# An S4 convolution and SwiGLU kernel: its order from the first feed-forward product on laid out by a planner in the source, and block products summed by accumulating transfers

## The chip, the core and the metric

The kernel runs on one core of a Trainium2 chip. A core has a matrix engine (TensorE, in the profile PE, its weight loads PEld), three engines for elementwise work (VectorE, in the profile DVE; ScalarE, ACT; GpSimd, POOL) and a queue engine that issues transfers (SyncE, SP). Sixteen DMA engines move data between the device memory and the on-chip memory, and within the latter. Each engine works through its own instructions in order and waits on semaphores for the others. The metric is the device time of one execution in microseconds.

## The reference

The input of 2048 rows by 512 features goes through two layers. Each adds a long convolution of the normalized rows, and then a gated feed-forward of the normalized result. Weights are the same in both layers.

```python
def _A_ref(u, A_re, A_im, B_re, B_im, C_re, C_im, log_dt, Dskip):
    dt = jnp.exp(log_dt)[:, None]
    logdA, dB = dt * (A_re + 1j * A_im), dt * (B_re + 1j * B_im)
    P = jnp.exp(logdA[:, :, None] * l[None, None, :])
    K = jnp.einsum("dn,dnl,dn->dl", Cc, P, dB).real
    ...
    Yf = Uf * Kf[None, :, :, :]
    y = irfft(Yf)[:L]
    return y + u * Dskip

def _B_ref(x, w_gate, w_up, w_down):
    return (silu(x @ w_gate) * (x @ w_up)) @ w_down

x = x + _A_ref(_layernorm(x), ...)
x = x + _B_ref(_layernorm(x), ...)
x = x + _A_ref(_layernorm(x), ...)
x = x + _B_ref(_layernorm(x), ...)
```

## The kernel before

The 2048 rows are four blocks of 512. With two layers there are eight block steps, in the order `SEQ`: (0,0), (0,1), (0,2), (1,0), (0,3), (1,1), (1,2), (1,3), as (layer, block). The text calls them step 0 to step 7. A step needs the spectra of the earlier blocks of its own layer, and for layer 1 the output of layer 0 for its block.

The first part, some 329 us, makes the convolution's kernel from its parameters, its spectra (`wdr` in device memory for the earlier blocks, `w0r` on chip for a block with itself), the spectra of blocks 0 and 1 of layer 0, and the convolution of step 0. DVE, ACT and PE stand there in the order of the source (`manual_schedule`). The change leaves this part as it is, up to the splitting of the feed-forward weights.

From the first feed-forward product on, each step has two halves of work.

The convolution (`ssm`, `forward`). A block is normalized, folded into lanes, and turned into spectra by products with a constant matrix (`pf`, line 276), which ACT copies to `u` (line 278); POOL stores them to `udr` (line 706) for later blocks. There are eight units per step: two halves of the features by four residues q. A unit multiplies its own spectrum by `w0r`, and that of each earlier block, loaded as `uu`, by a loaded `w`: one DVE product per block (line 755), each of 128 x 1024 numbers, and one DVE addition for each earlier block (line 758). Then come the joining of real and imaginary parts (lines 759 and 760), the split into a high and a low half-precision part (ACT line 763, DVE line 232), the products back (`pi`, line 774), and the combination of four units into the rows (`t1`, `t2`, `xt`, lines 791 to 807).

The feed-forward (`ffn`, `ffn_norm`, `remainder`). 256 rows at a time: a half block. The rows are normalized (ACT lines 223 to 226, a power on POOL line 227, DVE line 228), split into high and low parts and transposed by SP's transfers (line 840). Five groups of 48 products of 256 columns (`pgu`, lines 885 to 887) and one smaller group for the remaining 96 columns (lines 852 to 854) make gate and up. Each group is evicted by four instructions, in turns on ACT and DVE (lines 890 to 893). Then the second product `py` follows, two rows of 128 with 33 products each (lines 899 to 901); each row is added to `xt` by DVE (line 904) and stored by SP (line 906). `pgu` and `py` share two buffers of tag `big`.

Every product is made of three half-precision ones (high by high, high by low, low by high). So the weights are split too: ACT writes the high part (lines 641 and 667), DVE the low part (lines 646 and 670). These splits run on into the first feed-forward.

In this part the source gives only a program order. The framework's scheduler, with a timeline of its own, orders the instructions of every engine; evictions and the convolution's products have a raised priority (`BOOST`).

Of the kernel before, what the change touches and what calls it, by code (L numbers as in the profile page):

```python
# [11 lines left out]
F32 = mybir.dt.float32  # L12
# [29 lines left out]
HALF = 2  # L42
INV = 1
# [38 lines left out]
def kernel(ctx, tc, x, a_re, a_im, b_re, b_im, c_re, c_im, log_dt, d_skip,  # L82
# [10 lines left out]
                xf=1, nn=1, hh=1, hl=1, sg=2, hf=1, stats=2, stats2=2, ef=1)  # L93
# [38 lines left out]
    w0r = sb.tile([P, 2, 4, 2, HD], F32, name="w0r")  # L132
# [106 lines left out]

    def norm_x(n):  # L240
        rs, nb = row_stats(n, 4, 1.0, "stats", lambda r: tl([P, D], "junk", "t1", BF16))
        for c in range(4):
            A.activation(n[:, c], n[:, c], AF.Identity, scale=rs[:, c:c + 1], bias=nb[:, c:c + 1])

    def forward(n, h, eh):


        hs = slice(h * HD, (h + 1) * HD)
        x0, x1, x2, x3 = (n[:, c, hs] for c in range(4))
        bt = tl([P, 7, HD], "bt", "bt")  # L250
        a_, b_, p_, q_, r_, s_, hx = (bt[:, i] for i in range(7))
        stt(a_, x2, HH, x0, OP.add)
        stt(b_, x2, -HH, x0, OP.add)
        A.activation(hx, x2, AF.Copy, scale=HH)
        stt(p_, x3, TT, x1, OP.add)
        stt(r_, x3, -TT, x1, OP.add)
        stt(q_, x1, TT, x3, OP.subtract)
        stt(s_, x1, TT, x3, OP.add)
        for i, q in enumerate(QORD):
            z = z2[:, 0 if eh else i % 2]  # L260
            u_, v_ = ((p_, a_) if q in (0, 3) else (q_, b_))
            stt(z[:, 0], u_, CC if q < 2 else -CC, v_, OP.add)
            stt(z[:, 1], s_ if q in (0, 3) else r_, CC, hx, OP.add if q < 2 else OP.subtract)
            if eh:
                hl = z2[:, 1].bitcast(F16).rearrange("p i (l d) -> p l i d", l=2)
                A.activation(hl[:, 0], z, AF.Copy, scale=256.0)
                stt(hl[:, 1], z, 256.0, hl[:, 0], OP.subtract)
            pf = psml([P, 2, HD], "pf")
            with tc.high_priority(offset=BOOST):
                for o in range(2):  # L270
                    if eh:
                        terms = [(eh[:, q, o + i, le], hl[:, lz, i]) for i in range(2) for le, lz in ((0, 0), (0, 1), (1, 0))]
                    else:
                        terms = [(ef[:, q, o + i], z[:, i]) for i in range(2)]
                    for k, (e, m) in enumerate(terms):
                        PE.matmul(pf[:, o], lhsT=e, rhs=m, start=k == 0, stop=k == len(terms) - 1)  # L276
                u = tl([P, 2, HD], "u", "u")
                A.activation(u, pf, AF.Copy, scale=2.0 ** -16 if eh else 1.0)  # L278
            yield q, u
# [400 lines left out]
    def inputs():  # L680

        for layer, b in SEQ:
# [160 lines left out]
    def remainder(pgu, nh, nlo, hh, hl):  # L843

        rows = TB // P
        fs = slice(F - FR, F)
        pr = pgu.rearrange("p a b t -> p (a b t)")[:, :rows * 2 * FR].rearrange("p (r w f) -> p r w f", r=rows, w=2)
        for r in range(rows):
            rc = slice(r * P, (r + 1) * P)
            for wi in range(2):  # L850
                for k in range(4):
                    PE.matmul(pr[:, r, wi], lhsT=nh[:, k, rc], rhs=wgu(wi, k, 0)[:, fs], start=k == 0, stop=False)
                    PE.matmul(pr[:, r, wi], lhsT=nh[:, k, rc], rhs=wgu(wi, k, 1)[:, fs], start=False, stop=False)
                    PE.matmul(pr[:, r, wi], lhsT=nlo[:, k, rc], rhs=wgu(wi, k, 0)[:, fs], start=False, stop=k == 3)
        with tc.high_priority(offset=BOOST):
            both = tl([P, 2, TB], "sgr", "sg")
            sg = both[:, 0, :rows * FR].rearrange("p (r f) -> p r f", r=rows)
            hs = both[:, 1].bitcast(F16).rearrange("p (l r f) -> p l r f", l=2, r=rows)
            G.memset(hs[:, :, :, FR:], 0.0)
            A.activation(sg, pr[:, :, 0], AF.Silu, scale=sc6[:, 3:4])  # L860
            V.scalar_tensor_tensor(sg, pr[:, :, 1], sc6[:, 4:5], sg, OP.mult, OP.mult)
            A.activation(hs[:, 0, :, :FR], sg, AF.Copy)
            V.tensor_tensor(hs[:, 1, :, :FR], sg, hs[:, 0, :, :FR], OP.subtract)
            for i, o in enumerate((hh, hl)):
                for r in range(rows):
                    nc.sync.dma_start_transpose(o[:, FT - 1, r * P:(r + 1) * P], hs[:, i, r])

    def ffn(layer, b, ready=None):
        for s in range(T // TB):
            rows = TB // P  # L870
            xt = xs[SEQ.index((layer, b)) % 3][:, s * rows:(s + 1) * rows]
            nh, nlo = ready if ready and s == 0 else ffn_norm(layer, b, s)
            hh = tl([P, FT, TB], "hh", "hh", F16)
            hl = tl([P, FT, TB], "hl", "hl", F16)
            for f0 in (0, 2, 4, 6, FT - 1, 8) if ready and s == 0 else (FT - 1, 0, 2, 4, 6, 8):
                pgu = pbig([P, 2, 2, TB], "pgu")
                if f0 == FT - 1:
                    remainder(pgu, nh, nlo, hh, hl)
                    continue
                for i in range(2):  # L880
                    fs = slice((f0 + i) * P, (f0 + i + 1) * P)
                    for wi in range(2):
                        o = pgu[:, wi, i]
                        for k in range(4):
                            PE.matmul(o, lhsT=wgu(wi, k, 0)[:, fs], rhs=nh[:, k], start=k == 0, stop=False)  # L885
                            PE.matmul(o, lhsT=wgu(wi, k, 0)[:, fs], rhs=nlo[:, k], start=False, stop=False)  # L886
                            PE.matmul(o, lhsT=wgu(wi, k, 1)[:, fs], rhs=nh[:, k], start=False, stop=k == 3)  # L887
                with tc.high_priority(offset=BOOST):
                    sg = tl([P, 2, TB], "sg", "sg")
                    A.activation(sg, pgu[:, 0], AF.Silu, scale=sc6[:, 3:4])  # L890
                    V.scalar_tensor_tensor(sg, pgu[:, 1], sc6[:, 4:5], sg, OP.mult, OP.mult)  # L891
                    A.activation(hh[:, f0:f0 + 2], sg, AF.Copy)  # L892
                    V.tensor_tensor(hl[:, f0:f0 + 2], sg, hh[:, f0:f0 + 2], OP.subtract)
            py = pbig([P, rows, D], "py")
            for r in range(rows):
                rc = slice(r * P, (r + 1) * P)
                for f in range(FT):
# [26 lines left out]
    with tc.manual_schedule(engines={mybir.EngineType.Activation, mybir.EngineType.DVE, mybir.EngineType.PE}):  # L924
# [162 lines left out]
        def fetch(n):  # L1087
            for _ in range(n):
                if fetches:
                    fetches.pop(0)()  # L1090

        def split(hi, lo):
            for _ in range(hi):
                his.pop(0)()
# [97 lines left out]
```

## Time and profile before

| | |
|---|---|
| median of 3 runs | 1191.55 us (1190.38 to 1193.35) |
| the profiled execution, its own time | 1191.82 us |
| its span, first to last instruction | 1190.0 us |
| transfers, moved in the span | 146.91 MB, mean 123 GB/s |
| the chain that ended last, by engine | PE 48%, DVE 32%, ACT 9%, issue 6%, DMA 3% |

How to read the profile. A busy share is the time in which an engine had an instruction running; matmuls are pipelined, so a full PE may still have its products spaced wider than they need. A group of instructions has its line, engine, operation, the tiles it writes and reads, shape and count, then the total busy time and the mean of one in ns, and after the bar the idle time before them and what ended it. A row of the timeline has the start, the duration, engine, line and operation. A row of waits names the waiting instruction, the one waited for, the total, how often and the longest. The granted clock is the share of TensorE's full clock.

### The profile page before, as it was taken

What the parts mean: (1) busy time and instruction counts of PE and PEld (TensorE: products, weight loads), DVE (VectorE), ACT (ScalarE), POOL (GpSimd) and SP (SyncE); (2) the same over time, 40 slices, a digit from 0 to 9 for tenths busy, and PEclk for the clock granted to TensorE, in tenths of its full rate; (3) what the DMA queues carried; (4) which work ended last, traced back from release to release, by engine and by line L of the source; (5) the groups of instructions that cost most, each with busy time, mean ns of one, the idle gap of its engine ahead of it and who ended that gap; (6) DMA issues with size and microseconds to landing.
All of it is one profiled execution on the core that took longest, in us unless ns stands there. A gap on an engine that the chain in (4) does not pass through costs nothing.

```text
span 1190.0 us, 25245 instructions
## 1 busy us (share of the span) xinstructions
PE 1108.1 (93%) x10268; PEld 859.4 (72%) x10268; DVE 1026.7 (86%) x1623; ACT 618.8 (52%) x1168; POOL 178.9 (15%) x233
## 2 busy tenths in 40 slices
PE   2979999889978998999999999999999999999998
PEld 2857766667866766777777686868677686877875
DVE  8989999996899989999999999998997899983211
ACT  6998788763255445357744263564533552334211
POOL 3105444432300011011010000210200010000000
PEclk9999999999979998999999999999999999999999
DMA  6454455568468326442334443432445144312000
GB/s 235 124 138 129 109 128 125 118 184 232 146 199 248 103 72 187 129 129 89 103 94 142 135 149 128 145 107 98 130 131 191 45 120 129 114 51 45 14 24 18
DMA packets 138471, 146.91 MB, mean 123 GB/s; under 512 B 77873, under 2 KB 87089, under 8 KB 138354
## 3 DMA queue, kind: packets, MB, share of 16 engines
q1 hardware_dynamic: 133490, 128.51, 35.7%
q0 software_dynamic: 4864, 16.78, 5.8%
q8 instruction: 80, 1.31, 0.5%
q14 instruction: 37, 0.30, 0.1%
HBM read 98.19 MB, written 28.31 MB: 106 GB/s over the span
## 4 chain that ended last, share of the span: by engine, by line
PE 48%; DVE 32%; ACT 9%; issue 6%; DMA 3%; POOL 1%; SPq 1%; DVEq 0%; ACTq 0%; POOLq 0%
PE pgu L885 8%; PE pgu L887 8%; PE pgu L886 8%; PE pi L774 4%; DVE t L755 4%; PE pw L552 3%; PE py L899 3%; PE py L900 3%; PE py L901 3%; PE pf L276 3%; DVE yk L758 2%; DVE z L232 2%; DVE yk L755 2%; DVE im L394 1%; DVE sg L891 1%
## 5 line engine op out<-in xcount | busy, mean ns | idle before, releaser
L885 PE MATMUL pgu<-mix,wsl 128*128 128x256 f16 x1280 | 352.2, 275 | 9.1 <-DVE sg L891 5.5
L886 PE MATMUL pgu<-mix,wsl 128*128 128x256 f16 x1280 | 352.1, 275 | 1.2 <-DVE mix L831 1.2
L887 PE MATMUL pgu<-mix,wsl 128*128 128x256 f16 x1280 | 351.9, 275 | 0.4 <-DVE wsl L646 0.4
L886 PEld LDWEIGHTS <-wsl 128*128 128x128 f16 x1280 | 126.1, 99 | 27.1 <-issue 10.5
L887 PEld LDWEIGHTS <-wsl 128*128 128x128 f16 x1280 | 126.1, 99 | 21.1 <-DVE wsl L646 3.6
L885 PEld LDWEIGHTS <-wsl 128*128 128x128 f16 x1280 | 126.1, 99 | 16.9
L899 PE MATMUL py<-wsl,hh 128*128 128x512 f16 (+1 forms) x352 | 133.6, 380 | 4.3 <-DVE xf L904 2.5
L901 PE MATMUL py<-wsl,hl 128*128 128x512 f16 (+1 forms) x352 | 133.5, 379 | 0.0
L900 PE MATMUL py<-wsl,hh 128*128 128x512 f16 x320 | 121.4, 379 | 0.0
L755 DVE TENSOR_TENSOR t<-uu,w 128x1024 f32<-128x1024 f32 x96 | 117.1, 1220 | 0.7 <-DMA uu<-udr 0.6
L758 DVE TENSOR_TENSOR yk<-yk,t 128x1024 f32<-128x1024 f32 x96 | 117.0, 1219 | 0.3
L890 ACT ACTIVATE sg<-pgu,sc 128x512 f32<-128x512 f32 x80 | 54.5, 682 | 104.2 <-PE pgu L887 97.6
L774 PE MATMUL pi<-yl,mix 128*128 128x256 f16 x672 | 92.3, 273 | 7.5 <-ACT yl L763 6.0
L552 PE MATMUL pw<-kt,ek 128*128 128x256 f32 (+2 forms) x420 | 98.5, 373 | 0.0
L891 DVE SCALAR_TENSOR_TENSOR sg<-pgu,sc,sg 128x512 f32<-128x512 f32 x80 | 59.7, 747 | 43.7 <-ACT sg L890 43.5
L892 ACT ACTIVATE hh<-sg 128x512 f16<-128x512 f32 x80 | 50.1, 626 | 76.6 <-DVE sg L891 76.5
L552 PEld LDWEIGHTS pw<-kt,ek 128*128 128x128 f32 x420 | 78.2, 195 | 9.7
L227 POOL TENSOR_TENSOR rs<-mv,mhalf 128x2 f32<-128x2 f32 (+1 forms) x21 | 39.3, 1870 | 255.1 <-ACT mv L226 240.6
L774 PEld LDWEIGHTS <-mix 128*128 128x128 f16 x672 | 65.3, 98 | 13.6 <-issue 1.8
L276 PE MATMUL pf<-z,eh 128*128 128x256 f16 x576 | 74.9, 275 | 0.0
L763 ACT ACTIVATE yl<-mix,sy 128x512 f16<-128x512 f32 x56 | 40.1, 717 | 63.4 <-DVE mix L760 63.3
L755 DVE TENSOR_TENSOR yk<-u,w0r 128x1024 f32<-128x1024 f32 x56 | 68.3, 1220 | 0.3 <-ACT u L278 0.3
(250 smaller groups left out, 2232.6 us busy)
## 6 DMA issues: line engine op xcount, KB each, us to landing
w<-wdr SPq DMA_DIRECT2D x96, 256.0 KB, 2.7
uu<-udr SPq DMA_DIRECT2D x96, 256.0 KB, 3.0
udr<-u POOLq DMA_DIRECT2D x32, 256.0 KB, 2.4
wdr<-wo SPq DMA_DIRECT2D x96, 64.0 KB, 2.3
udr<-u SPq DMA_DIRECT2D x16, 256.0 KB, 2.5
g<-tmp POOLq DMA_DIRECT2D x8, 512.0 KB, 4.7
g<-btl POOLq DMA_DIRECT2D x8, 512.0 KB, 6.1
n<-xdr SPq DMA_DIRECT2D x4, 1024.0 KB, 5.7
```

Source lines behind the costliest of these rows:

```text
L276: PE.matmul(pf[:, o], lhsT=e, rhs=m, start=k == 0, stop=k == len(terms) - 1)
L552: PE.matmul(pw[:, i], lhsT=e, rhs=kt[:, :, c + 4 * k0:4 * k1:4, :].rearrange("p g k d -> p k g d"), start=c == 0, stop=c == 3)
L755: V.tensor_tensor(t, uu.unsqueeze(1).to_broadcast([P, 2, 2, HD]), w.unsqueeze(2).to_broadcast([P, 2, 2, HD]), OP.mult)
L758: V.tensor_tensor(yk, yk, t, OP.add)
L774: PE.matmul(pi[:, o], lhsT=e, rhs=m, start=k == 0, stop=k == len(terms) - 1)
L885: PE.matmul(o, lhsT=wgu(wi, k, 0)[:, fs], rhs=nh[:, k], start=k == 0, stop=False)
L886: PE.matmul(o, lhsT=wgu(wi, k, 0)[:, fs], rhs=nlo[:, k], start=False, stop=False)
L887: PE.matmul(o, lhsT=wgu(wi, k, 1)[:, fs], rhs=nh[:, k], start=False, stop=k == 3)
L891: V.scalar_tensor_tensor(sg, pgu[:, 1], sc6[:, 4:5], sg, OP.mult, OP.mult)
L899: PE.matmul(py[:, r], lhsT=hh[:n, f, rc], rhs=wd(f, 0)[:n], start=f == 0, stop=False)
L900: PE.matmul(py[:, r], lhsT=hh[:n, f, rc], rhs=wd(f, 1)[:n], start=False, stop=False)
L901: PE.matmul(py[:, r], lhsT=hl[:n, f, rc], rhs=wd(f, 0)[:n], start=False, stop=f == FT - 1)
```

## The change

The function `inputs` now serves step 0 alone, and `norm_x`, `forward`, `remainder` and the loop over `SEQ` at the end are replaced. In their place functions `plan_...` describe every piece of work as a job: its engine, an assumed duration, the jobs it depends on, a priority, the buffers it takes (`get`) and gives back (`put`), and a function that issues it. `emit` then plays a list schedule through: at each turn it takes the engine whose next job can begin first, and of that engine's jobs that can begin then, the one with the smallest priority; it issues the job and books its assumed end. All of it stands inside `manual_schedule`, so DVE, ACT and PE keep exactly this order; SP and POOL do not belong to the engines named there.

```diff
+HOP = 150
+SLACK = 0.0
+LAND = 2000
+BUSY = dict(DVE=3300.0, ACT=1500.0)
+MARGIN = 1500.0
+ACC = 9000
+CAP = dict(w=3, uu=3, u=2, big=2, sg=2, pi=2, yl=2, bb=2, dd=2)
...
-    w0r = sb.tile([P, 2, 4, 2, HD], F32, name="w0r")
+    w0r = tl([P, 2, 4, 2, HD], "w0r", "w0")
...
+    def job(eng, ns, fn, deps=(), pr=(), get=(), put=(), lat=None):
+        j = dict(eng=eng, ns=ns, lat=ns + HOP if lat is None else lat, fn=fn, deps=[d for d in deps if d], pr=pr,
+                 get=[(k, len(took.setdefault(k, []))) for k in get], end=None)
...
+    def emit():
...
+        def earliest(j):
+            t = free.get(j["eng"], 0.0)
+            for d in j["deps"]:
+                if d["end"] is None:
+                    return None
+                t = max(t, d["end"] + (MARGIN if j["eng"] == "PE" and j["pr"][0] == 0 else 0))
...
+            return t
+
+        while any(left.values()):
+            best = None
+            for todo in left.values():
+                ready = [(earliest(j), j["pr"], n) for n, j in enumerate(todo[:400])]
+                ready = [r for r in ready if r[0] is not None]
+                if ready:
+                    t0 = min(r[0] for r in ready)
+                    t0, p, n = min((r for r in ready if r[0] <= t0 + SLACK), key=lambda r: (r[1], r[0], r[2]))
+                    if best is None or t0 < best[0]:
+                        best = t0, todo, n
+            t, todo, n = best
+            j = todo.pop(n)
+            j["fn"]()
+            free[j["eng"]] = t + j["ns"]
+            j["end"] = t + j["lat"]
+            if "bytes" in j:
+                pipe = max(pipe, t) + j["bytes"] / 300.0
+                j["end"] = pipe + j["lat"]
+
+    def dve(n, ps=False):
+        return n / 0.96 + (128 if ps else 68)
+
+    def act(n, acc=False):
+        return n * 0.833 + (161 if acc else 68)
+
+    def dma(kb, fn, deps=(), pr=(), get=(), put=()):
+        j = job("SP", 350, fn, deps, pr, get, put, 2300)
+        j["bytes"] = kb * 1024
+        return j
```

The weight splits get priority (0, 0, k) on ACT and (0, 1, k) on DVE, their loads (0, k) on SP. The convolution of step i gets (1, i, ...) on DVE and ACT, with (0, i, ...) for its products on PE. The groups of the feed-forward get (1, i, s, gi) on PE, for half s and group gi; their evictions get (0, 0, i, s, gi).

The convolution's sums. For the first two earlier blocks the product is added into the sum `yk` by a transfer that accumulates, issued by POOL; for a third one DVE adds as before. After step 1 the tile of `w0r` (16 KB in each partition) becomes four buffers for products and sums, so that there are three of each; `w0r` is first stored to `wdr[0]` (two transfers of 1 MB, `evict`), and the weights of a block with itself are loaded from there for steps 2 to 7. In step 1 two sums are held, in the tiles of `z` and `y1`.

```diff
+                if k or i > 1:
+                    def load_w(c=c, k=k, h=h, q=q):
+                        c["w"] = tl([P, 2, HD], "w", "w")
+                        nc.sync.dma_start(c["w"], wdr[k, h, q])
+                    deps.append(dma(256, load_w, () if k else evict, (3, i, n, k), ["w"]))
...
+                def add(c=c, o=o):
+                    G.dma_start(o["yk"], c["t"], accum_op=OP.add)
+
+                def plus(c=c, o=o):
+                    V.tensor_tensor(o["yk"], o["yk"], c["t"], OP.add)
...
+                j = job("DVE", dve(4 * HD), mult, deps, (1, i, 3, n, k), [key], put)
...
+                if k and k < 3:
+                    prev = job("POOL", 570, add, [j, prev], (1, i, n, k), (), [key], ACC)
+                elif k:
+                    prev = job("DVE", dve(4 * HD), plus, [j, prev], (1, i, 3, n, k), (), [key])
...
+    evict = [dma(1024, lambda h=h: nc.sync.dma_start(wdr[0, h].rearrange("q p i d -> p q i d"), w0r[:, h]),
+                 pr=(2,)) for h in range(2)]
```

The second product is issued in five pieces per row, each a job, with row 1 behind row 0; the eviction of a row is a job on DVE. The small group of 96 columns has a buffer of its own (`pr`) in place of one of tag `big`.

```diff
+            for r in range(rows):
+                for fl in ((0, 1), (2, 3), (4, 5), (6, 7), (8, 9, 10)):
+                    dep = [d for f in fl for d in ready[f // 2 * 2]] + [split.get(8 + f) for f in fl]
+                    prev = job("PE", len(fl) * 3 * 217, lambda f=mmd, r=r, fl=fl: f(r, fl), dep + [prev], (1, i, s, 9),
+                               ["big"] if r == 0 and fl[0] == 0 else (), ["hh"] if r == rows - 1 and fl[0] == 8 else (),
+                               len(fl) * 3 * 217 + 180)
...
+                def addx(r=r, c=s * rows + r, o=o):
+                    V.scalar_tensor_tensor(xs[i % 3][:, c], o["py"][:, r], sc6[:, 5:6], xs[i % 3][:, c], OP.mult, OP.add)
...
+                j = job("DVE", dve(D, True), addx, [prev], (0, 0, i, s, 9), (), ["big"] if r == rows - 1 else ())
```

The loop that remains:

```diff
-    for i, lb in enumerate(SEQ):
-        if i + 1 < len(SEQ):
-            take(itertools.chain(*ssm(*SEQ[i + 1])), 100)
-        ffn(*lb, ready if i == 0 else None)
+        for i in range(len(SEQ)):
+            if i + 1 == HALF:
+                ehj = dma(768, load_eh, pr=(2, 2), get=["ef"])
+            if i + 1 < len(SEQ):
+                plan_ssm(i + 1, ehj)
+            normed = [[] if i + s == 0 else plan_norm(i, s) for s in range(T // TB)]
+            plan_ffn(i, normed, split_jobs if i == 0 else {})
+        emit()
```

The number and shape of the products on PE, the normalizations, the evictions and the transposes stay as they were.

More of the change, by code (lines that the diff above doesn't have):

```diff
@@ L680, in inputs @@
     def inputs():
-        for layer, b in SEQ:
+        for layer, b in SEQ[:1]:
             if layer == 0 and b < 2:
@@ L841, in ffn_norm @@
         return nh, nlo
[L843 to L847, printed above, removed]
-        for r in range(rows):
[L849 to L866, printed above, removed]
```

511 lines of the change are left out of this document (423 added, 88 removed).

## The prediction

> **What bounds the kernel now.** The page first: span and busy shares.
>
> ```profile
> span 1190.0 us, 25245 instructions
> PE 1108.1 (93%) x10268; PEld 859.4 (72%) x10268; DVE 1026.7 (86%) x1623; ACT 618.8 (52%) x1168; POOL 178.9 (15%) x233
> ```
>
> PE and DVE are both nearly full, so shares do not say which one sets the end. A busy PE need not be at its peak either. I therefore worked out what its work costs at full rate, from the first feed-forward product on, where the change begins: counts from the groups of instructions, start-to-start times from rows of the timeline.
>
> ```profile
> L885 PE MATMUL pgu<-mix,wsl 128*128 128x256 f16 x1280 | 352.2, 275 | 9.1 <-DVE sg L891 5.5 <-DVE sgr L861 1.4 <-DMA wdr<-wo 1.1
> L774 PE MATMUL pi<-yl,mix 128*128 128x256 f16 x672 | 92.3, 273 | 7.5 <-ACT yl L763 6.0 <-DVE yl L232 1.5
> L276 PE MATMUL pf<-z,eh 128*128 128x256 f16 x576 | 74.9, 275 | 0.0
> L899 PE MATMUL py<-wsl,hh 128*128 128x512 f16 (+1 forms) x352 | 133.6, 380 | 4.3 <-DVE xf L904 2.5
> L852 PE MATMUL pgu<-wsl,mix 128*128 128x96 f16 x256 | 37.8, 209 | 3.2 <-DMA mix<-nn 2.7 <-DVE sg L891 0.5
> ...
> 329.29 0.37 PE L885 MATMUL pgu<-mix,wsl 128*128 128x256 f16 x1 [1.11 <-DMA wdr<-wo]
> ...
> 1101.89 0.27 PE L885 MATMUL pgu<-mix,wsl 128*128 128x256 f16 x1
> ...
> 1128.09 0.38 PE L899 MATMUL py<-wsl,hh 128*128 128x512 f16 x1
> ...
> 1178.71 0.38 PE L899 MATMUL py<-wsl,hh 128*128 128x512 f16 x1 [0.84 <-DVE xg L904]
> ...
> 1185.62 0.38 PE L901 MATMUL py<-wsl,hl 96*128 96x512 f16 x1
> ...
> 1135.50:1137.20 1.70, 1.70 (x41) 1.69 (x40) 0.75 (x1) 0.00 (x0) 0.00 (x0) 1.00 0.00 0
> ```
>
> Between 1101.89 and 1128.09 stand the 240 products of one half block: 0.1092 us each. Between 1178.71 and 1185.62 stand 32 steps of the 512-wide form: 0.216. The last row is a window (its columns are told below) that holds 41 products of the 96-wide form and nothing else, in 1.70 us: 0.0415. Lines L886, L887, L900, L901, L853 and L854 repeat the counts of their neighbours. So 3 x 1280 + 672 + 576 = 5088 at 0.1092 is 555.6; 3 x 352 = 1056 at 0.216 is 228.1; 3 x 256 = 768 at 0.0415 is 31.9: **816 us of work**. From 329.3 to the last product's end at 1186.0 there are 856.7 us. PE loses about **40 us**, and the rest of this stage is PE's own work, which the change leaves as it is. The windows say where the 40 lie (columns: length, then busy time of PE, PEld, DVE, ACT, POOL with counts, granted clock, DMA share, GB/s).
>
> ```profile
> 329.00:480.00 151.00, 133.79 (x1088) 102.83 (x1088) 141.63 (x230) 78.44 (x140) 10.21 (x12) 0.92 0.54 162
> 480.00:1050.00 570.00, 560.31 (x4759) 435.60 (x4758) 541.88 (x895) 267.89 (x521) 48.23 (x53) 1.00 0.39 120
> 1050.00:1190.00 140.00, 135.15 (x1070) 98.90 (x1067) 45.27 (x73) 35.06 (x64) 2.05 (x4) 1.00 0.10 26
> ...
> 329.00:336.00 7.00, 5.47 (x26) 3.73 (x26) 6.43 (x7) 5.91 (x6) 0.00 (x0) 0.51 1.03 342
> 349.60:356.40 6.80, 5.37 (x25) 3.59 (x25) 6.75 (x8) 2.77 (x8) 1.81 (x1) 0.50 0.38 130
> 370.10:373.50 3.40, 3.05 (x15) 2.12 (x15) 3.40 (x6) 2.31 (x5) 0.00 (x0) 0.50 0.78 201
> 452.00:458.80 6.80, 4.29 (x35) 3.46 (x36) 6.80 (x12) 3.27 (x7) 0.00 (x0) 0.50 0.76 227
> ```
>
> Before 480: 151 - 133.8 = 17 us without a product, and four stretches at half clock, 24 us long, which lose 12: **29 us**. From 480 on: 9.7, and 140 - 135.2 less the 4 us after the last product, 0.9: **10.5 us**. DVE is 95% busy there (541.88 of 570), yet PE hardly waits. Relief of DVE is therefore worth at most 10.5 us after 480; the larger prize is the 29 us at the start.
>
> The Trainium skill, "TensorE: Matmul & The Clock Gate", section "What's actually happening", lets the clock fall to half after an idle window of about 3.4 us. The half-clock stretches here are 3.4 or twice 3.4 us long, in agreement, though the one at 349.6 came with a wait below that. By that rule the stops of about 1 us that I forecast below keep full clock, as the 1.00 from 480 on also has it.
>
> **The change part by part.**
>
> *Order at the start.* What PE waited for before 480:
>
> ```profile
> PEld L887 <- DVE wsl L646: 3.6, 1, 3.6
> PE pgu L885 <- DVE sg L891: 5.1, 2, 4.3
> PE pi L774 <- ACT yl L763: 3.9, 2, 2.7
> PE pgu L854 <- DMA mix<-nn: 2.8, 2, 2.2
> PE pgu L852 <- DMA mix<-nn: 2.7, 1, 2.7
> ...
> 331.80 1.43 ACT L641 ACTIVATE wsl<-xg,sc 128x1376 f16<-128x1376 f32 x1
> 350.42 0.93 DVE L646 SCALAR_TENSOR_TENSOR wsl<-xg,sc,wsl 128x688 f16<-128x688 f32 x1
> ```
>
> ACT wrote the high part of a weight tile at 331.8, but DVE made its low part only at 350.4, behind products and sums of the convolution. The weights held PE for 3.6 us (a convolution product in front of them waited 2.7 of these for its own operand), and the half clock at 349.6 took 3.4. The planner puts splits (0, 1, k) ahead of convolution work (1, i, ...), and convolution products on PE 1.5 us behind their data. The next stop, 4.3 us for an eviction that DVE made late, with 1.7 of half clock at 370, also goes: evictions get (0, 0, ...). That is 3.6 + 3.4 + 4.3 + 1.7 = 13 us. The first product's cold clock, 3.4 us, and a wait of 1.1 (its row) with some 0.5 behind it stay: 5 us. The rest, 1.2 + 2.8 + 2.7 = 6.7 us with 3.4 of clock at 452, comes from block 1's sums and norms being late. Block 1 loses 8 additions, 9 us of DVE, but its sums now go through transfers with two accumulators; I keep 3 us (ends 0 and 10). What is late next is DMA: it was at 1.03 of its engines at 329, and two stores of 1 MB (`evict`) and eight accumulations join the w_down loads. I charge 4 us, one more stop like that at 370 with less clock (ends 0, and 17 for two of the old size with half clock). Start after: 5 + 3 + 4 = **12 us** against 29 (ends 5 and 32).
>
> *Additions moved off DVE.* The blocks after the first have 1, 2, 0, 3, 1, 2, 3 earlier blocks, so 8 x 12 = 96 additions; the first two of a sum move, 8 x 10 = 80, and 16 stay.
>
> ```profile
> L755 DVE TENSOR_TENSOR t<-uu,w 128x1024 f32<-128x1024 f32 x96 | 117.1, 1220 | 0.7 <-DMA uu<-udr 0.6
> L758 DVE TENSOR_TENSOR yk<-yk,t 128x1024 f32<-128x1024 f32 x96 | 117.0, 1219 | 0.3
> ...
> g<-tmp POOLq DMA_DIRECT2D x8, 512.0 KB, 4.7
> g<-btl POOLq DMA_DIRECT2D x8, 512.0 KB, 6.1
> ...
> q0 software_dynamic: 4864, 16.78, 5.8%
> ...
> 47.77 1.08 POOL L500 DMA_DIRECT2D g<-tmp  x1 [12.59 <-DVE tmp L499]
> 47.93 1.21 DVE L503 TENSOR_TENSOR g<-g,xr 128x1024 f32<-128x1024 f32 x1
> ```
>
> 80 x 1.219 = 98 us leave DVE of the 684 it has from 329 to 1050; since PE waits little there, the gain is a part of the 10.5 us. An accumulating transfer of this size lands after 4.7 or 6.1 us; the plan allows 9 (`ACC`). Its engine time is bounded by the software queue: 5.8% of 1190 us is 69 us for 16.78 MB, half of it accumulated: 2.2 us each at the mean rate, 4.3 if all were theirs. 80 of them add 173 to 345 us to engines that were at 0.54 and 0.39; with 48 more weight loads they come to some 0.65 to 0.85. That is below full, with the head room at the start smallest. POOL pays up to 1.1 us per issue, 86 in all, out of its idle 85%. On POOL a second accumulation waits for the first one's landing; behind it stand the norms' powers and the stores of spectra. The plan's 9 us cover that, so I put nothing.
>
> Does the issue slow DVE? At 47.77 POOL issues such a transfer while DVE's product of two SBUF tiles takes 1.21, its usual time: no. The Trainium skill, "SBUF — State Buffer", section "Who interferes with whom", has an exclusive lock between GpSimd's reads and a DVE instruction with two SBUF inputs. If issuing held it, up to 86 us would come back to DVE; the row shows none of it.
>
> *Row handover in the second product.* This is what I expect to cost. `py` holds two rows; the row above at 1178.71 waited 0.84 us for L904, which evicts row 0, although row 1 is written to another half of the tile. In that half block nothing stood between the rows. Elsewhere the old order put other products there, and the waits come to 4.3 us in total (row L899). In the new order row 1's pieces (1, i, s, 9) come ahead of the next half's (1, i, s + 1, ...); only a convolution product that is ready just then covers the wait. 16 convolution products fall on 85 us of feed-forward per block, so about 7 of 16 handovers are covered, and 9 pay 1.0 us each (the step of 1.2 us less 0.2): 9 us. Ends: 0, if the wait does not come back when pieces are interleaved, and 16 x 1.7 = 27 when DVE is in mid-product.
>
> *The other waits after 480*, 10.5 less about 3.6 of handovers, 7 us: the plan places convolution products 1.5 us late (`MARGIN`) and DVE has room; I keep 3 (ends 0 and 10).
>
> **Sum.** 12 + 9 + 3 = 24 us of loss against 40 (41 by the first count, 39.5 by the windows): 16 less. The profiled execution took 1191.8 us, 1.8 beyond its span and 0.3 above the median of 1191.55: 1191.8 - 16 = **1175.8**.
>
> **Rivals.**
> *Handover free.* If row 1 need not wait, 9 us go as well: 1167. For: the two rows are different bytes. Against: the wait in the row at 1178.71.
> *The start is not mended.* DMA is the bound there, weights or block 1's sums land late, and PE falls to half clock again: 26 us of loss instead of 12, so 1190. For: the share of 1.03 at 329. Against: 0.38 to 0.78 in the three later stretches.
> *Slower: sums late in a fixed DVE order.* DVE runs in the planned order. If an accumulation takes more than 9 us, the join of its sum stands at the head of DVE, and evictions behind it. A group of products takes 48 x 0.109 = 5.2 us; its eviction is an ACT and a DVE instruction of 0.7 us each (rows below). So some 3.7 us are covered: it decides from 12.7 us. Beyond that 48 sums with accumulation each cost PE what is over. At 13.5 us that is 48 x 0.8 = 38: 1176 + 38 = 1214; with half of them on an eviction, 1195. I name 1205. Against: 4.7 and 6.1 us measured. For: more load than then; a weight load below took 11.1 us where its fellow took 6.0.
>
> ```profile
> L890 ACT ACTIVATE sg<-pgu,sc 128x512 f32<-128x512 f32 x80 | 54.5, 682 | 104.2 <-PE pgu L887 97.6
> L891 DVE SCALAR_TENSOR_TENSOR sg<-pgu,sc,sg 128x512 f32<-128x512 f32 x80 | 59.7, 747 | 43.7 <-ACT sg L890 43.5
> ...
> st<-in_B_w_gate_dram SPq DMA_DIRECT2D x2, 688.0 KB, 6.0
> spare<-in_B_w_up_dram SPq DMA_DIRECT2D x2, 688.0 KB, 11.1
> ```
>
> *It does not do what it says.* POOL and SP stay outside the planned engines, so their order may undo the plan: 1191.
>
> **How the numbers follow.** Forecast 0.50, handover free 0.16, start not mended 0.16, slower 0.15, no effect 0.03. About 0.3%, 3.6 us, is what a measurement here can tell from no change. Faster: 0.48 + 0.16 + 0.06 = 0.70; same: 0.02 + 0.08 + 0.03 = 0.13; slower: 0.15 + 0.02 = 0.17. The floor, with nothing but the cold start lost, is 1191.8 - 35 = 1157; the range goes from 1160 to 1197, the unmended start and the cheap part of the slower case included.
>
> **What would show it.** Right: no stop of PE behind a weight split or an eviction before 460; DVE some 90 us less busy between 329 and 1050; some ten PE waits of about 1 us for the eviction of row 0. Wrong: accumulations landing after more than 9 us with DVE waiting for them; granted clock under 1 after 480; the sum of PE waits after 480 well over 12 us.

## The result, and the profile after

The changed kernel is **slower**: 1265.57 us (median of 6 runs, 1260.26 to 1277.74) against 1193.53 (6 runs, 1190.38 to 1195.56), a ratio of 1.062 [1.057, 1.067]. The prediction said 1175.8, with a range that ended at 1197. The profiled execution took 1271.73 us, 79.9 more than that of before. The page of after, span and busy shares:

```profile
span 1270.0 us, 25376 instructions
PE 1131.3 (89%) x10268; PEld 867.4 (68%) x10268; DVE 956.6 (75%) x1543; ACT 614.8 (48%) x1168; POOL 232.7 (18%) x313
```

DVE was busy 70 us less, and the kernel became 80 us longer. (The 80 instructions that went are 98 us by their length. But instructions back to back overlap by some 0.08 us in the records, and after a wait they do not, so the busy time fell by less.) PE has the same 10268 products. Summed from 329 on at the full-rate spacings of the prediction, they are again some 816 us. From 329 to the end of the last product at 1266 there are 937 us, so PE now loses about 122 us; before it was about 41. The same windows as before (length, busy time of PE, PEld, DVE, ACT and POOL with counts, granted clock, DMA share, GB/s), with the longest stretch of low clock and one more:

```profile
329.00:480.00 151.00, 124.94 (x1022) 95.33 (x1021) 119.20 (x199) 76.24 (x148) 21.56 (x28) 0.90 0.75 208
480.00:1050.00 570.00, 521.90 (x4315) 402.02 (x4313) 439.00 (x765) 246.54 (x482) 79.52 (x107) 0.97 0.71 178
1050.00:1270.00 220.00, 204.20 (x1577) 147.74 (x1574) 98.56 (x151) 51.68 (x93) 10.76 (x16) 0.97 0.33 82
...
445.00:466.00 21.00, 8.73 (x55) 6.28 (x55) 12.33 (x21) 5.92 (x14) 3.87 (x6) 0.51 1.04 271
490.00:497.00 7.00, 5.85 (x30) 4.23 (x30) 6.96 (x11) 4.21 (x7) 1.44 (x2) 0.53 0.80 265
```

The stretch from 480 to 1050 shows it best. Before, PE stood 9.7 of its 570 us without a product, with DVE at 541.88 busy. Now PE stands 48 us, and DVE has only 439: both wait. The DMA share rose from 0.39 to 0.71. The stretches at half clock add up to some 79 us from 329 on, 24 before. PE had a product running in 56 of them, 18 before, so the low clock itself cost some 28 us against 9; the other 94 (32 before) are stops.

Who waits for what, from 329 on (waiting instruction, released by, total us, times, longest):

```profile
PE pgu L1262 <- DVE sg L1277: 27.2, 16, 6.3
PE py L1298 <- DVE xg L1310: 12.2, 6, 3.9
...
DVE sg L1277 <- ACT sg L1274: 82.4, 31, 13.2
DVE nn L1182 <- DMA mix<-nn: 25.8, 6, 7.6
DVE yt L1048 <- DMA w<-wdr: 24.2, 10, 4.1
DVE yk L1048 <- DMA w<-wdr: 15.1, 3, 7.5
DVE t L1048 <- DMA w<-wdr: 6.5, 2, 4.8
DVE mix L1069 <- DMA yk<-t: 2.6, 3, 1.5
```

PE waits for evictions (L1277), as it did before for L891, but 27 us in place of 5.5. DVE waits 46 us for weights (24.2 + 15.1 + 6.5) and 26 for a transpose to read a normalized tile. In before it has no row of waits for `w`, and for the transposes this one:

```profile
DVE nn L838 <- DMA mix<-nn: 1.7, 2, 1.1
```

For an accumulated sum DVE waits 2.6 us. The long first DVE row is the echo: an eviction whose products were themselves late. One such stop on DVE's timeline of after, and the product on PE that waited for it (start, duration, engine, line, operation, in brackets the idle time before it and its releaser):

```profile
480.46 0.68 DVE L239 SCALAR_TENSOR_TENSOR z<-z 128x512 f16<-128x512 f32 x1
487.63 0.69 DVE L1182 TENSOR_TENSOR nn<-nn 128x512 f16<-128x512 f32 x1 [6.49 <-DMA mix<-nn]
...
490.36 0.74 DVE L1277 SCALAR_TENSOR_TENSOR sg<-pgu,sc,sg 128x512 f32<-128x512 f32 x1
...
491.15 0.37 PE L1262 MATMUL pgu<-mix,wsl 128*128 128x256 f16 x1 [6.35 <-DVE sg L1277]
```

DVE stands from 481 on before the split of a normalized tile, whose buffer a transpose still reads. The eviction at 490.36 is behind it in the fixed order. So PE stood still 6.35 us from 484.8 on, and the clock was at about half from 490 to 497 (0.53 in the window above). The Trainium skill, "TensorE: Matmul & The Clock Gate", section "What's actually happening", has this fall after an idle window of some 3.4 us; the trace agrees, for here the clock fell some 5 us into the stop. Where the prediction had seen only stops of about 1 us after 480, which keep full clock, these are the long kind. Now the transfers, of after, on the page (bytes, median us from issue to landing; queues: packets, MB, share of 16 engines):

```profile
w<-wdr SPq DMA_DIRECT2D x144, 256.0 KB, 4.5
uu<-udr SPq DMA_DIRECT2D x96, 256.0 KB, 4.5
yt<-yt POOLq DMA_DIRECT2D x41, 512.0 KB, 6.9
yk<-yt POOLq DMA_DIRECT2D x17, 512.0 KB, 6.5
yk<-t POOLq DMA_DIRECT2D x14, 512.0 KB, 6.0
...
q0 software_dynamic: 16384, 58.73, 23.6%
```

In before, the same loads took:

```profile
w<-wdr SPq DMA_DIRECT2D x96, 256.0 KB, 2.7
uu<-udr SPq DMA_DIRECT2D x96, 256.0 KB, 3.0
```

Most accumulations land inside the 9 us that the plan allows (3 of the 80 do not, the longest took 10.0). But the software queue took 23.6% of 1270 us, 300, where it took 69 before: 231 us of packet time for 80 accumulations, **2.9 us of all sixteen engines each**. The share of 0.71 between 480 and 1050 is a mean: of the 57 stretches of 10 us in it, 17 are at 0.90 or more, while in before the highest is 0.78. (The share adds up the time of packets, so it can pass 1.) Weight loads beside them went from 2.7 to 4.5 us, and the chain that ended last, in order of time, holds loads of 7.7 to 8.1 (start, length, what):

```profile
1068.12 7.91 DMA w<-wdr
...
1083.84 7.65 DMA w<-wdr
1091.52 1.23 DVE yt L1048
1092.74 0.67 DVE xf L1310
1093.46 0.27 PE pgu L1262
1103.42 8.11 DMA w<-wdr
```

### The profile page after: what moved, and what is told of

It is laid out like the page before. It is cut to its first block, busy times and chain, and to the rows that moved or that the text cites. A ratio compares the mean times of both kernels' runs of the same rounds, so it can differ in the third digit from the quotient of the medians.

```text
span 1270.0 us, 25376 instructions
## 1 busy us (share of the span) xinstructions
PE 1131.3 (89%) x10268; PEld 867.4 (68%) x10268; DVE 956.6 (75%) x1543; ACT 614.8 (48%) x1168; POOL 232.7 (18%) x313
## 3 DMA queue, kind: packets, MB, share of 16 engines
q0 software_dynamic: 16384, 58.73, 23.6%
## 5 line engine op out<-in xcount | busy, mean ns | idle before, releaser
L1263 PEld LDWEIGHTS <-wsl 128*128 128x128 f16 x1280 | 127.4, 100 | 57.6 <-issue 34.5
L1298 PE MATMUL py<-wsl,hh 128*128 128x512 f16 (+1 forms) x352 | 136.2, 387 | 26.9 <-DVE xg L1310 12.2
L1262 PEld LDWEIGHTS <-wsl 128*128 128x128 f16 x1280 | 127.4, 100 | 23.7 <-DVE sg L1277 0.2
L1264 PEld LDWEIGHTS <-wsl 128*128 128x128 f16 x1280 | 127.5, 100 | 18.5 <-issue 1.5
L1300 PE MATMUL py<-wsl,hl 128*128 128x512 f16 (+1 forms) x352 | 136.1, 387 | 0.0
L1299 PE MATMUL py<-wsl,hh 128*128 128x512 f16 x320 | 124.1, 388 | 4.4 <-DVE wsl L636 4.4
L1277 DVE SCALAR_TENSOR_TENSOR sg<-pgu,sc,sg 128x512 f32<-128x512 f32 x80 | 59.6, 748 | 82.4 <-ACT sg L1274 82.4
L1084 PE MATMUL pi<-yl,mix 128*128 128x256 f16 x672 | 84.7, 275 | 8.3 <-ACT yl L1073 5.0
L984 PE MATMUL pf<-z,eh 128*128 128x256 f16 x576 | 74.8, 280 | 16.7 <-DVE z L239 10.4
L984 PEld LDWEIGHTS <-eh 128*128 128x128 f16 x576 | 57.7, 100 | 28.8 <-issue 18.5
L1048 DVE TENSOR_TENSOR yt<-uu,w 128x1024 f32<-128x1024 f32 x58 | 70.7, 1219 | 8.2 <-DMA w<-wdr 8.2
L1299 PEld LDWEIGHTS <-hh 128*128 128x128 f16 (+1 forms) x352 | 35.0, 99 | 59.2 <-issue 32.0
L1052 POOL DMA_DIRECT2D yt<-yt x41 | 36.2, 882 | 205.4 <-DVE yt L1048 124.8
```

What stands on the lines that cost most here:

```text
L984: PE.matmul(pfs[:, o_], lhsT=e, rhs=z, start=k == 0, stop=k == len(terms) - 1)
L1048: V.tensor_tensor(t, u.unsqueeze(1).to_broadcast([P, 2, 2, HD]), w.unsqueeze(2).to_broadcast([P, 2, 2, HD]), OP.mult)
L1084: PE.matmul(pis[n % 2][:, o_], lhsT=e, rhs=m, start=k == 0, stop=k == len(terms) - 1)
L1262: PE.matmul(d, lhsT=wgu(wi, k, 0)[:, fs], rhs=nh[:, k], start=k == 0, stop=False)
L1263: PE.matmul(d, lhsT=wgu(wi, k, 0)[:, fs], rhs=nlo[:, k], start=False, stop=False)
L1264: PE.matmul(d, lhsT=wgu(wi, k, 1)[:, fs], rhs=nh[:, k], start=False, stop=k == 3)
```

## The experiments

Two causes were on the table. **Load**: 80 accumulations fill the DMA engines, and loads that a fixed DVE order counts on come late. **Order**: the plan itself is worse than the framework's order, with or without the accumulations, because its assumed durations are wrong, or because SP and POOL are outside it. Times below are medians; brackets hold the 95% interval of the ratio to before, taken beside it. Each diff is against the changed kernel unless it says otherwise.

**e1 and e2: fewer accumulations.** e1 leaves all 96 additions on DVE; e2, with `k < 2` in the line below, keeps one accumulation per sum (48 in place of 80).

```diff
-                if k and k < 3:
+                if k and k < 1:
```

> All 96 additions stay on DVE, as before the change; order planner, buffers and the extra weight loads stay as after. If the accumulating transfers cost the time (their load on the DMA engines makes loads land late and DVE stand in its fixed order), the DMA share between 480 and 1050 us falls from 0.71 to about 0.45, weight loads land in 3 us instead of 4.5, and the time falls to 1180 to 1215 us. If the planned order itself costs it, the time stays within 1245 to 1290 us, or rises, since DVE has 98 us more.

> Only the first addition of a sum goes by transfer: 48 instead of 80, so 32 are back on DVE. If the accumulating transfers cost the time, the dose shows: about two thirds of the loss stay with DMA load, some 1225 to 1250 us, and less if the second transfer of a sum (which waits for the first) is the costly one. If the order costs it: 1255 to 1285 us.

e1: 1237.06, 1.037 [1.032, 1.041]. e2: 1239.78, 1.039 [1.034, 1.044]. Without any accumulation the plan is still 3.7% slower than before, between the two cases that had been expected; the accumulations add 28 us on top, although they take 98 us from DVE. The first one of each sum costs nothing that shows, the 32 second ones cost it all (DMA share from 480 to 1050 in e1, e2 and after: 0.47, 0.62, 0.71; weight loads 3.0, 3.8, 4.5 us). A second one also has to wait on POOL for the first, so this pair of runs does not separate the load from that wait. The larger part of the loss is the order, with the 48 further weight loads of the change in it. One place where it comes about, in e1, on SP's timeline, then on DVE's and PE's:

```profile
643.43 2.45 SPq L1241 DMA_TRANSPOSE hh<-sgr  x2
645.97 2.46 SPq L1241 DMA_TRANSPOSE hl<-sgr  x2
...
650.09 2.63 SPq L1175 DMA_TRANSPOSE mix<-nn  x2
652.81 0.53 SPq L1028 DMA_DIRECT2D w<-wdr  x1
```

```profile
651.09 1.22 DVE L1055 TENSOR_TENSOR yt<-yt,t 128x1024 f32<-128x1024 f32 x1
656.32 1.23 DVE L1048 TENSOR_TENSOR yt<-uu,w 128x1024 f32<-128x1024 f32 x1 [4.02 <-DMA w<-wdr]
...
659.27 0.74 DVE L1277 SCALAR_TENSOR_TENSOR sg<-pgu,sc,sg 128x512 f32<-128x512 f32 x1
...
660.07 0.27 PE L1262 MATMUL pgu<-mix,wsl 128*128 128x256 f16 x1 [4.27 <-DVE sg L1277]
```

A transpose holds SP for 1.2 us while it is issued (two take 2.45 here). The plan books 0.1 (`job("SP", 100, ...)`). So the weights were issued only at 652.81, DVE stood 4 us, the eviction came at 659.27, and PE stopped for 4.3 us.

**e3 and e4: SP and POOL in the planned order too**, with accumulations (e3) and without (e4).

```diff
-        emit()
+        with tc.manual_schedule(engines={..., mybir.EngineType.SP, mybir.EngineType.Pool}):
+            emit()
```

> SP and POOL follow the planned order too, from the first planned job on. If the framework's own order of SP and POOL against a fixed DVE, ACT and PE order costs the time (transposes and weight loads behind transfers that wait), the waits of ACT and DVE for transposes, 60 us in all, shrink to under 20, and the time falls by 30 us or more. If DMA load costs it, the time moves by less than 15 us.

> Both at once: SP and POOL in the planned order, all additions on DVE. If the two causes are separate and add up, the gains of the two single kernels add up. If only DMA load counts, it is as fast as the kernel with DVE additions alone; if only the queue order counts, as the one with SP and POOL planned.

e3: 1297.88, 1.088 [1.072, 1.103], 32 us more, which neither case had expected. e4: 1233.94, 1.034 [1.029, 1.038], as e1. That two engines keep an order of their own is not what costs: binding SP to the plan's wrong times makes it worse or leaves it.

**e5, e6, e7: the transposes at their price.** e5 without accumulations, e6 with them, e7 as e5 with SP and POOL in the plan.

```diff
-            a = job("SP", 100, lambda r=r: turn(r, 0), [j], (0, i), ..., lat=2600)
+            a = job("SP", 1200, lambda r=r: turn(r, 0), [j], (0, i), ..., lat=3700)
...
-                             ready[f0].append(job("SP", 100, lambda t=turn, k=k, r=r: t(k, r), ..., 2600))
+                             ready[f0].append(job("SP", 1200, lambda t=turn, k=k, r=r: t(k, r), ..., 3700))
```

> All additions on DVE, and the planner books a transpose at 1200 ns of SP and 3700 ns to landing, in place of 100 and 2600 (the traces have 1.2 us of SP for each). If the plan's wrong price for SP's transposes is what throws DVE's fixed order out (weight loads issued late behind eight transposes per half block), the time falls from 1237 to 1190 to 1210 us, and DVE's waits for weight loads and transposes, 22 us, to under 8. If other errors of the plan carry it, it stays over 1225 us.

> The kernel after with the same two prices corrected, transfers still accumulating. If the transposes' price is the main cause of the order's loss and the accumulations cost the rest, 1225 to 1245 us; if the accumulations' load only hurts because the plan is off, under 1215 us; if the price does not matter, about 1266 us.

> As the first of this call, with SP and POOL in the planned order as well. With the price right the planned order of SP should now fit: 1190 to 1210 us if the theory of the price holds, and no worse than the first. If SP's own order by the framework was the better one, it is slower than the first by 10 us or more.

e5: 1217.48, 1.020 [1.015, 1.026], 20 us less than e1 by this price alone, though not yet the 1210 that had been expected of it. e6: 1259.14, 1.055 [1.046, 1.064]: with the accumulations nearly nothing of it is left. e7: 1209.81, 1.014 [1.009, 1.019]. The group of waits that had been 27 to 28 us, in e1 and then in e7:

```profile
PE pgu L1262 <- DVE sg L1277: 28.1, 15, 6.7
```

```profile
PE pgu L1262 <- DVE sg L1277: 10.1, 12, 2.5
```

**e8, e9, e13, e17, e18: what is left of the order.** e8 is e5 with row 1 of the second product placed behind the small group of the next half block. e9 is e7 with this, and with ACT and load durations as the trace has them. e13 is e9 without the eviction of `w0r` and its reloads, with one buffer each for products and sums. e17 and e18 are e9 with `MARGIN` doubled, and at 600.

```diff
-                    ..., dep + [prev], (1, i, s, 9),
+                    ..., dep + [prev], (1, i, s, 9) if r == 0 else (1, i + s, 1 - s, 0.5),
...
-        return n * 0.833 + (161 if acc else 68)
+        return n * 0.833 + (320 if acc else 145)
...
-        j = job("SP", 350, fn, deps, pr, get, put, 2300)
+        j = job("SP", 420, fn, deps, pr, get, put, 2700)
```

> As the first of this call, but the pieces of row 1 of the second product get a priority behind the small group of the next half block, so that these products lie between the two rows. If the handover of the rows costs about 1 us in most of the 16 half blocks, the waits of the second product for the eviction of row 0 fall from 6.4 us to under 3 and the time by 3 to 12 us. If not, it moves by under 3 us.

> All additions on DVE, SP and POOL in the planned order, row 1 behind the next small group, and prices set from the traces: transposes 1200 and 3700 ns, ACT 77 ns more per instruction (159 with an accumulator), loads 420 ns to issue and 400 more to land. If a fixed order loses only by the plan's wrong prices, this reaches 1190 to 1203 us. If a fixed order without transfers' help has a loss of its own that prices do not mend, it stays at 1205 us or above.

> As the kernel with all prices set (1197), but the weights of a block with itself stay on chip: no stores of 1 MB, 48 loads of 256 KB fewer, and one buffer each for sum and product again, as before the change. If less DMA load is worth more than the buffers, 1185 to 1195 us; if the buffers are needed to keep DVE going, 1200 us or more.

> The best planned kernel with convolution products booked 3.0 instead of 1.5 us behind their data. If PE's remaining stops come from products placed too soon, 1188 to 1195 us; if they come from evictions that DVE makes late and from the start, within 3 us of 1197.

> The best planned kernel with convolution products booked 0.6 instead of 1.5 us behind their data. The larger lead of 3.0 us cost 21 us. If that was because the convolution's chain falls behind when its products wait, a smaller lead gains: 1185 to 1194 us. If 1.5 us is near the best, since PE then stops for products placed too soon, 1195 to 1208 us.

e8: 1211.54, 1.015 [1.007, 1.023]; its interval overlaps that of e5, and the waits of `py` for an eviction of a row did not fall (9.1 + 1.8 us after 7.7 + 2.7): undecided. e9: 1197.09 (10 runs), **1.001 [1.000, 1.003]**, level with before. e13: 1200.85, 1.006 [1.004, 1.008]; so keeping `w0r` on chip, with the fewer buffers that leaves, gains nothing. e17: 1218.47, 1.020 [1.015, 1.025]. e18: 1194.21 (10 runs), 1.001 [0.999, 1.003]. A margin of 3 us on convolution products costs 21 us, which neither case of its expectation had; one below 1.5 brings nothing that can be told from e9. The windows of e9:

```profile
329.00:480.00 151.00, 133.17 (x1126) 103.58 (x1125) 142.85 (x227) 79.62 (x148) 8.11 (x12) 0.96 0.67 203
480.00:1050.00 570.00, 557.25 (x4717) 432.00 (x4714) 538.27 (x881) 264.05 (x510) 41.00 (x53) 1.00 0.46 137
```

With prices from the trace, SP and POOL in the plan and row 1 moved, the plan does what the framework did: 12.8 us without a product after 480 (9.7 before), DVE as full as it was. And at the start PE still stands 17.8 us, 17.2 before, though at a granted clock of 0.96, not 0.92.

**e10 and e16: is the load harmless once it is booked?** e10 is e6 with e9's durations, and with the accumulation's engine time and that of POOL's stores of spectra in the plan's model of the DMA pipe; e16 is e9 with the accumulations back and their engine time booked.

```diff
-                    prev = job("POOL", 570, add, [j, prev], (1, i, n, k), (), [key], ACC)
+                    prev = job("POOL", 900, add, [j, prev], (1, i, n, k), (), [key], ACC - 2900)
+                    prev["bytes"] = 870000
```

> Transfers accumulate as in the changed kernel, with the transposes, ACT and loads priced as above, and the planner's one DMA pipe now also books each accumulation (2.9 us of all engines) and each store of spectra. If accumulations hurt because the plan does not see the DMA time that they take, it falls from 1259 to 1220 us or less. If they hurt by that DMA time itself, whatever the plan, it stays at 1240 us or more.

> The best planned kernel (1197 us: prices set from the traces, SP and POOL planned, row 1 behind the next small group) with the 80 accumulations back, their DMA time booked. It gives the price of the accumulations in the mended plan: 1235 us or more if it is their load, which the plan cannot remove; under 1210 us if the earlier loss came from the plan's errors together with them.

e10: 1248.77, 1.045 [1.041, 1.048]. e16: 1251.20, 1.047 [1.040, 1.055], 54 us above e9. So the accumulations cost more in a good plan than in the bad one (54 us, and 28 between e1 and the change). A plan that knows of their engine time gets little of it back: e10 is 10 us below e6, with intervals that overlap, and it has e9's durations besides. The windows of e16, beside those of e9 above:

```profile
329.00:480.00 151.00, 116.14 (x897) 85.81 (x895) 112.58 (x188) 65.26 (x118) 17.58 (x24) 0.86 0.85 230
480.00:1050.00 570.00, 542.88 (x4574) 421.93 (x4573) 457.21 (x795) 266.35 (x523) 87.15 (x111) 0.99 0.77 185
```

From 480 to 1050 DVE is busy 81 us less, and PE stands 27 us there, not 12.8; at the start it stands 35, not 17.8, and at a lower clock.

**e11, e12, e14, e15: the load alone.** At each of the 80 places of an accumulation POOL copies a few numbers of the product and then starts a copy of 1 MB from device memory to device memory, whose result nothing uses; all additions stay on DVE. e11 does this in e7, e12 in the kernel before; e15 and e14 are the same without the 1 MB, that is without the second line.

```diff
+                        G.tensor_copy(tiny, t[:, 0, 0, :16])
+                        G.dma_start(dump[next(dumps)], c_dump)
```

> The kernel with DVE additions, priced transposes and SP and POOL planned (1210 us), plus a copy of 1 MB in device memory that nobody waits for, at each of the 80 places where the change has an accumulation; a small POOL copy in front makes it wait for the product. The copies' results are not used. If the load on the DMA engines is what the accumulations cost, the time rises to 1235 us or more and weight loads land in over 4 us. If the cost is the sums' waiting for their own transfers, the time stays under 1218 us.

> The kernel before, in the framework's order, with the same 80 copies of 1 MB in device memory, each behind a small POOL copy that reads the product. The copies' results are not used. If DMA load of this size harms whatever the order, it loses as much as the planned kernel did, 50 us or more (1245 or over). If it is the fixed plan that makes the load harmful, it loses less than 20 us.

> Control for the kernel before with the copies: the small POOL copies alone, no transfers. The product's buffer is held until POOL has read it, and there is only one. If the copies' load is what counts, this stays within 10 us of the kernel before; what it loses is to be taken off the loss with the copies.

> Control for the planned kernel with the copies: the small POOL copies alone, no transfers. If the load is what cost 80 us there, this stays within 10 us of 1210; what it loses is to be taken off.

| order | without (e15, e14) | with 80 copies (e11, e12) | cost |
|---|---|---|---|
| plan of e7 | 1208.28, 1.011 [1.009, 1.014] | 1290.34, 1.079 [1.073, 1.086] | 82 us |
| framework | 1194.29, 1.000 [0.999, 1.001] | 1216.57, 1.018 [1.014, 1.022] | 22 us |

The small copies alone cost nothing (e15 as e7, e14 as before). The software queue of e11 and of e12:

```profile
q0 software_dynamic: 16384, 100.67, 24.3%
```

```profile
q0 software_dynamic: 16384, 100.67, 25.6%
```

That is 312 us in both (24.3% of 1282.7 and 25.6% of 1217.7), 241 above the 70 without copies: 3.0 us each, close to the 2.9 of an accumulation. **The same load on the DMA engines harms either kernel, and the planned one nearly four times as much.** The window from 480 to 1050 of e11, then of e12:

```profile
480.00:1050.00 570.00, 511.95 (x4167) 390.64 (x4166) 477.20 (x784) 240.48 (x473) 115.45 (x159) 0.95 0.70 219
```

```profile
480.00:1050.00 570.00, 551.24 (x4655) 429.16 (x4654) 518.24 (x864) 265.51 (x517) 131.79 (x170) 1.00 0.74 226
```

The DMA share is as high in the framework's order, and weights land in 4.2 us there, in 4.9 in e11. DVE waits 41 us for weights in e11 (30.0 and 10.8) and in e12 for none of the loads of `w`. Why the planned kernel suffers more is not settled. The framework's scheduler laid out its order with the copies in it, while the plan of e11 booked only their issue on POOL; e16 speaks against much of this, for there the time was booked. The traces show another difference. If each load of `w` is paired, in order, with the product that reads it, the kernel before issues a load 16.6 us ahead of its product (median; a tenth of them under 11.5), e12 17.5 (12.4), but e11 only 12.2 (6.7): the change sends 144 loads through the three buffers of `w` that had 96. e13 has a planned order too, but keeps `w0r` on chip, and its lead is 16.2 (11.5), as before. So the short lead comes with the reloads of `w0r` and not with planning as such. A plan without the reloads and with the copies was not run, so what each is worth is not shown.

No version was shown to be faster than before.

## Why the prediction was wrong

*What bounds it.* PE's work stayed at 816 us, as forecast. That relief of DVE is worth little was not tested alone: e16 takes 81 us from DVE after 480 and PE waits more there, but with the load on the DMA engines as well.

*"The start: 12 us against 29."* Wrong, and the rival "the start is not mended" was right about this place, though not shown to be right about its cause. The 29 was itself too high by 3: PE had a product running in only 18 of the 24 us at half clock, so these lost 9, not 12. In after, PE stands 26 us before 480 with the clock at 0.90; in e9, with right prices and no accumulation, it still stands 17.8, as long as in before, at 0.96. The DMA share there is 0.75 with accumulations and 0.67 without, against 0.54, but that DMA is what holds the start up was not tested. In e9 most of the start's waits are short ones for weight splits, a transpose and the convolution, and none is for an eviction longer than 2 us (its list of PE's waits before 480):

```profile
PE py L1299 <- DVE wsl L636: 4.2, 5, 2.3
PE pr L1219 <- DMA mix<-nn: 3.8, 1, 3.8
PE pi L1084 <- DVE yl L239: 3.4, 2, 2.2
...
PE pgu L1262 <- DVE sg L1277: 2.0, 2, 1.8
```

So the two long stops that the plan was to remove went, and others took their place, five of them for splits of the `w_down` weights. Whether any order mends the start stays open.

*"That is below full"*, and *"The plan's 9 us cover that, so I put nothing."* This is the first step that failed. The engine time was forecast well (2.2 to 4.3 us each, measured 2.9) and so was the share (0.65 to 0.85; 0.75 and 0.71). I compared that mean share with 1, though it is made of full and empty stretches, and asked only whether the sums would be late. They hardly are: 6.0 to 6.9 us by the medians, 3 of 80 over 9, and DVE waits 2.6 us for them. What is late is what else uses the same engines: weights at 4.5 in place of 2.7 us, up to 8 on the chain that ended last. Price: 28 us in the change as made, 42 once transposes are priced (e6 less e5), 54 in the mended plan (e16 less e9). I counted the 48 further weight loads only in that share, too, and not that they shorten the lead from a load's issue to its use (10.4 us in e9 with them, 16.2 in e13 without).

*"The other waits after 480 ... I keep 3."* The second step that failed, and by e1 the larger: 44 us with no accumulation at all. Of the 122 us that PE loses in the changed kernel, some 35 lie before 480 and 15 at the handovers of rows, so this term came to some 70, not 3. I read the plan's priorities and margins, and did not hold its assumed durations against the trace. This group of transposes of before stood in it (line, operation, count, shortest, median and longest ns):

```profile
L840 SPq DMA_TRANSPOSE mix<-nn x60: 1189/1211/2350, 363.2 to 1091.3; - x60
```

The plan has 100. With the 64 of `hh` and `hl` that is 124 x 1.1 = 136 us of SP that it does not know of. This price alone is worth 20 us (e5 less e1); with SP and POOL, the row, ACT's and the loads' prices, 40 (e9 less e1). What each of these last is worth was not separated, but together they bring the order back to before.

*"It does not do what it says", 0.03.* Too low, and for the wrong reason: SP and POOL outside the plan would have been this rival's cause, and e3 and e4 show that binding them does not help while the plan's prices are wrong; the plan's own errors are what undid it.

*The slower rival* had the right engine and the right victim, evictions behind a DVE instruction that waits, and the wrong trigger: a sum later than 9 us. What came late was not the sum but, above all, the loads beside it and the buffers behind the transposes, and for these it had set no price.

*Row handover, 9 us.* The price of one was right. The waits for L1310 came to 12.2 + 3.1 = 15.3 us in 7 waits, against 4.3 in 6 before. In a half block with nothing between the rows, the chain of after has:

```profile
1220.53 0.23 PE py L1300
1220.79 0.76 DVE xg L1310
1221.59 0.38 PE py L1298
```

About 1.0 us, as priced; in the others the waits are longer, behind a late DVE. In e5, where DVE is less late, there are 10 waits with 10.4 us in all, close to the 9 of 1.0 that the prediction had. e8, meant to free the rows, did not lower them.

*Issuing does not slow DVE.* Right: with 80 accumulations issued by POOL, the 58 products of one kind take 1219 ns each, 1220 before. The lock of the Trainium skill's page "SBUF — State Buffer", section "Who interferes with whom", is not seen in an issue here either.

## What to carry to other kernels

Before you trust an order written by a planner, put each of its assumed durations beside the trace, those of the queue engine first: one price of 0.1 us for 1.2 cost 20 us, and right prices, with SP and POOL in the plan and row 1 moved, only brought it back to where the framework's order had been. A transfer that saves an engine's work is paid for by all sixteen DMA engines, so ask what else lands later, not when the transfer itself lands. The same copies cost the planned kernel 82 us, whose weight loads are issued some 12 us ahead of their use, and the kernel before 22, where it is 17; whether this lead is the reason was not tested.

## What was not expected of the hardware

An accumulating transfer of 512 KB within on-chip memory took 2.9 us of all sixteen DMA engines, as much as a copy of 1 MB within device memory (3.0). A load of 256 KB went from 2.7 us at a mean DMA share of 0.39 to 4.5 at 0.71. That mean is short of full, but nearly a third of its stretches of 10 us hardly are (17 of 57 at 0.90 or more; 6 in e2, none in before). And the first accumulation of each sum was free in time (e2 against e1), while 32 more cost 26 us, between mean shares of 0.62 and 0.71.
